# Attention and gated MLP on one core: PV placed beside score visits, output scaling and key masks on POOL, x held in two chunks

## The chip, the cores and the metric

The kernel runs on one core of a Trainium2 chip. A core has a matrix engine (TensorE, PE in the profile, with its weight loads as PEld), a vector engine (DVE), a scalar engine (ACT), a third elementwise engine (POOL), a queue engine (SP) that issues DMAs here, an on-chip memory of 128 partitions (SBUF) and eight accumulation banks of 128 x 512 fp32 (PSUM). The engines run their own instruction lists in order and wait for each other by semaphores. The metric is the device time of one execution in microseconds.

## The reference

There are 2,048 tokens of width 512. Two branches see the same x and are mixed per token by a gate. All tensors are bf16.

```python
x = A_x
g = sigmoid((x * gate_w).sum(-1))
a = A(x)          # 32 heads of 16, 4 segments of 512 tokens
b = B(x)          # gated MLP with 1,792 hidden units
out = g * a + (1 - g) * b

# A, per segment s, per head:
logits = q @ k.T * 16**-0.5 + causal mask      # 512 x 512, inside the segment
a_dot = softmax(logits) @ v
a_mem = (phi(q) @ M) / (phi(q) @ z + 1e-6)     # phi(t) = t + 1 for t > 0, else exp(t)
o = sigmoid(beta) * a_mem + (1 - sigmoid(beta)) * a_dot
M += phi(k).T @ v;  z += sum(phi(k))           # for the later segments
# then o @ wo

# B:
gate = x @ W_gate;  up = x @ W_up
return (gate * (gate > 0) * up) @ W_down
```

## The kernel before, in words

**Who decides the order.** `program` describes every piece of work as an `Op`: the engines that may do it, a cost for each, the resources that it reads and writes. `Sched.run` then walks a model of time: again and again it takes, of all queue heads, the one that can start first (queues have priorities, ties are broken by a seeded random number), puts it on its engine's list and notes the semaphore waits it needs. `Sched.emit` writes the lists out. So the order on each engine is fixed when the program is built, and a change of a cost, a buffer or a rule shifts all of it. PSUM accumulators are `Epoch`s: a bank is chosen when the first matmul of an epoch is placed and is free again when its readers are done.

**Projections** (`proj`, L671 and L673). Per segment, q and k are projected transposed (features on partitions), v token by token; 48 matmuls of 512 columns. DVE or ACT evicts them (L678, L682, L686, L699). The key masks (`kmask`, L690 on DVE, L691 on ACT) copy kT twice into `kp`, each time with half of the features of a head pair set to zero. For the memory, phi(q) and phi(k) are formed (L655 to L657) and phi(k) is transposed by DMA (L696).

**Score visits** (`quad`, L775). A group G holds 8 heads. Keys are taken in chunks of 64, and causality leaves chunk c with 512 - 64c query columns. A visit fills four PSUM banks of `psL` with 512 columns for each of four 32-row strips of TensorE: chunk 0 alone, chunks 1 and 7, 2 and 6, 3 and 5, and chunk 4 of two neighbouring groups. That makes 18 visits per segment. ACT takes the exponential of all 2,048 columns at once (L781) into one of eight blocks of `E` (seven in rotation, one kept for chunk 4), and POOL zeroes the triangles with four selects per visit (L786).

**PV** (L809). When all visits of a group are masked, 128 narrow matmuls multiply E by v, with a column of (1 + exp(beta)) for the denominator, into two banks. The half of v that sits on the other partitions is copied by DMA (`vsh`, L757). DVE transposes both banks into `Tn` (L819), takes the reciprocal (L827), multiplies in the gate (`rdg`, L829), scales into `adT` (`ad`, L831), transposes back (L834 or L836) and adds the memory part (L837) into `oT`. In the scheduler a PV belongs to a mode of TensorE of its own and is tied to a visit of the next group (`pair[0].gate = pes[k]`).

**Memory** (`mu`, L716 to L725; `nd`, L736 to L748): one update per segment, and four small matmul groups with a division per later segment.

**MLP** (`ffn`, L874 to L885; `outp`, L906 to L923). Per segment, 14 hidden blocks of 128: four gate and four up matmuls each, a relu (ACT L882 or DVE L883) and a product (DVE L885) into 16 slots `hT`. The output accumulates 14 matmuls with W_down (L913) and 4 with wo (L906) in one bank, and the eviction multiplies by 1 - g.

**x.** The transposed x, `xT`, holds all four chunks of 512 tokens. Chunk 0 is transposed by TensorE, chunks 1 to 3 come by transposing DMA (`load_x`, L506) on SP early on.

Of the kernel before, what the change touches and what calls it, by code (L numbers as in the profile page):

```python
# [15 lines left out]
MU_G = 1  # L16
PE_LAT = 175.0
SWITCH = 100.0
GATE_T = {1: 44000.0, 2: 90000.0, 3: 140000.0}

# [29 lines left out]
class Epoch:  # L50
    _n = 0

    def __init__(self, cls="mid", nb=1):
        self.nb = nb
        self.group = (self,)
        Epoch._n += 1
        self.res = f"ACCep{Epoch._n}"
        self.bank = None
        self.readers = []
        self.cls = cls  # L60


class Op:
    __slots__ = ("engs", "eng", "fns", "occs", "lat", "reads", "writes", "name", "dma", "nbytes", "mode", "ep", "role",
                 "after", "nbk", "port", "base", "preds", "stream", "idx", "start", "end", "done", "cidx", "gate", "nd")

    def __init__(self, alts, reads=(), writes=(), name="", lat=0.0, dma=False, nbytes=0, mode="f", ep=None, role=None):
# [18 lines left out]
        self.gate = None  # L86
        self.nd = 1
# [10 lines left out]
class Sched:  # L98
# [3 lines left out]
    def __init__(self, ndma=16, nbanks=4, seeds=(0,)):  # L102
        self.seeds = seeds
        self.jit = {}
        self.bank_ep = [None] * nbanks
# [88 lines left out]
    def pv_due(self):  # L194
        q = self.queues["pe"][self.pvq]
        while q[2] < len(q[1]) and q[1][q[2]].done:
            q[2] += 1
        if q[2] >= len(q[1]) or q[1][q[2]].gate is None:
            return 0
        t = self.now["pe"] + 500.0  # L200
        return q[1][q[2]].nbk if all(p.done and p.end <= t for p, _ in q[1][q[2]].preds) else 0

    def _bank_choice(self, op, e):
        cls, nb, n = op.ep.cls, op.ep.nb, len(self.bank_ep)
        idle = [p is None or all(r.done for r in p.readers) for p in self.bank_ep]
        if cls != "att":
            held = sum(not f and p.cls == cls for f, p in zip(idle, self.bank_ep))
            if held + nb > self.CAPS.get(cls, 2) or (n - sum(idle) + nb > n - max(self.pv_due(), 1) if nb == 1 else sum(idle) < (2 if self.relax else 3)):
                return None
        best = None  # L210
        for bi in range(n - nb + 1):
            if not all(idle[bi:bi + nb]):
                continue
            ft = max(self._bank_free(p, e) for p in self.bank_ep[bi:bi + nb])
            key = ft
            if nb == 1 and cls == "att" and n == 4:
                m = self.bank_ep[bi ^ 1]
                key += 0.0 if idle[bi ^ 1] or (m is not None and m.cls == "att") else 200.0
            if best is None or key < best[2]:
                best = (bi, ft, key)  # L220
        return best and best[:2]

# [6 lines left out]
    def ready(self, op, e):  # L229
        t0 = self.now[e]  # L230
        t = op.after
        if op.gate is not None:
            if self.mode != "r" and not op.gate.done:
                return None
            if sum(p is None or all(r.done for r in p.readers) for p in self.bank_ep) < op.nbk:
                return None
            t = max(t, sorted(self._bank_free(p, e) for p in self.bank_ep if p is None or all(r.done for r in p.readers))[op.nbk - 1])
# [5 lines left out]
        if op.ep is not None:  # L243
            if op.role == "w" and op.ep.bank is None:
                for rd in op.ep.readers:
                    for p, _ in rd.preds:
                        if p.ep is op.ep or p.cidx > op.cidx:
                            continue
# [3 lines left out]
                bc = self._bank_choice(op, e)  # L252
# [24 lines left out]
    def place(self, op, e, start):  # L277
        op.eng = e
        if op.ep is not None and op.role == "w" and op.ep.bank is None:
            for ep in op.ep.group:  # L280
                bi, _ = self._bank_choice(op, e)
# [45 lines left out]
        op.stream, op.idx, op.start, op.done = st, idx, start, True  # L327
        sn = dict(self.know[e])
# [7 lines left out]

    def jitter(self, op):
        seed = self.seeds[min(int(self.now["pe"] / 34000.0), len(self.seeds) - 1)]
# [5 lines left out]
    def _choose(self, e):  # L344
        heads = []
        for q in self.queues[e]:
# [6 lines left out]
            if rt is not None:  # L353
                pr = q[0]
                if e in ("dve", "act") and op.ep is not None and op.role == "r" and sum(p is None or all(r.done for r in p.readers) for p in self.bank_ep) < 2:
                    pr = min(pr, 0.5)
                heads.append((pr, rt, op))
        if not heads:
            return None
        now = self.now[e]  # L360
# [48 lines left out]
def plan(S, D, F):  # L409
    NT, KT, NF = S // 128, D // 128, F // 128  # L410
    return [
        ("xT", [128, KT, S], BF16), ("wq", [128, KT, 512], BF16), ("wk", [128, KT, 512], BF16), ("wv", [128, KT, 512], BF16),
        ("wo", [128, 4, 512], BF16), ("wg", [128, KT, F], BF16), ("wu", [128, KT, F], BF16), ("wd", [128, NF, 512], BF16),
        ("qT", [128, 8, 512], BF16), ("kT", [128, 4, 512], BF16), ("kp", [128, 5, 8, 128], BF16),
        ("phiq", [128, 4, 512], BF16), ("ek", [128, 4, 512], BF16), ("phik", [128, 4, 512], BF16), ("ttmp", [128, 2, 512], BF16),
        ("vaug", [128, 2, 4, 32, 17], BF16), ("vsh", [128, 4, 32, 17], BF16), ("E", [128, 8, 4, 512], BF16),
        ("Tn", [128, 2, 512], F32), ("adT", [128, 512], BF16), ("oTt", [128, 512], BF16),
        ("amem", [128, 2, 512], BF16), ("amemT", [128, 4, 512], BF16), ("oT", [128, 8, 512], BF16),
        ("hT", [128, 16, 512], BF16), ("rl", [128, 3, 512], BF16), ("osb", [128, 3, 512], BF16),
# [3 lines left out]
        ("rden", [128, 32], F32), ("rdg", [128, 32], F32), ("rdm", [128, 128], F32), ("pm8", [128, 8], F32), ("pm", [128, 2], F32), ("ident", [128, 128], BF16),  # L423
# [3 lines left out]
def build_kernel(nc, A_x, A_wq, A_wk, A_wv, A_wo, A_beta, W_g, W_u, W_d, gate_w, out):  # L427
# [5 lines left out]
    sc = Sched(seeds=(52936,98560,17166,30259,57195,44848,1710,92264))  # L433
    T = {}
    with contextlib.ExitStack() as stack:
        for name, shape, dt in plan(S, D, F):
            T[name] = stack.enter_context(nc.sbuf_tensor(name, shape, dt))
        PL = stack.enter_context(nc.psum_tensor("psL", [128, 4, 512], F32))
        PA = stack.enter_context(nc.psum_tensor("psA", [128, 4, 512], F32))
        for st in sc.streams:  # L440
            sc.sem[st] = stack.enter_context(nc.semaphore(f"s_{st}"))
        program(sc, nc, T, PL, PA, A_x, A_wq, A_wk, A_wv, A_wo, A_beta, W_g, W_u, W_d, gate_w, out, NSEG, KT, NF, NT, EPS, SCALE)
# [4 lines left out]

def program(sc, nc, T, PL, PA, A_x, A_wq, A_wk, A_wv, A_wo, A_beta, W_g, W_u, W_d, gate_w, out, NSEG, KT, NF, NT, EPS, SCALE):
    V = type("V", (), T)

# [24 lines left out]
    def A(ep):  # L475
        return PA[:, ep.bank, :] if ep.nb == 1 else PA[:, ep.bank:ep.bank + 2, :]

    def xt(c):
        return [f"xT{c}_{kt}" for kt in range(KT)] if c else [f"xT0_{i}" for i in range(6)]
# [24 lines left out]
    def load_x(c):  # L504
        for kt in range(KT):
            lsp.append(dma("sp", lambda e, c=c, kt=kt: e.dma_start_transpose(V.xT[:, kt, c * 512:(c + 1) * 512], A_x[0, c * 512:(c + 1) * 512, kt * 128:(kt + 1) * 128]),  # L506
                           1 << 17, occ=1280.0, writes=[f"xT{c}_{kt}"], name=f"ldx{c}_{kt}"))
# [39 lines left out]
    for b in range(4):  # L547
        ds.append(dve(lambda e, b=b: e.memset(PA[:, b, :], 0.0), 500, writes=[f"init{b}"], name=f"init{b}"))
# [100 lines left out]
    def qslot(s, G):  # L649
        return (s % 2) * 4 + G  # L650

    def phi(s, px, G, dst, dn, src, slot, rd, acts, sbs):
        xv, pv = src[:, slot:slot + 2, :], dst[:, G - 1:G + 1, :]
        wr = [f"{dn}{G - 1}", f"{dn}{G}"]
        acts.append(act(lambda e: e.activation(pv, xv, ACT.Exp), t_act(1024, False), reads=rd, writes=wr, name=f"{px}exp{s}_{G}"))  # L655
        sbs.append(dve(lambda e: e.tensor_scalar(V.ttmp[:, :, :], xv, 0.0, 1.0, ALU.max, ALU.add), 400, reads=rd, writes=["ttmp"], name=f"{px}ts{s}_{G}"))
        sbs.append(dve(lambda e: e.tensor_tensor(pv, pv, V.ttmp[:, :, :], ALU.min), 700, reads=wr + ["ttmp"], writes=wr, name=f"{px}phi{s}_{G}"))  # L657

    def proj(s):
        pes, evs, sbs, acts, sps = [], [], [], [], []  # L660
        tok = s * 512
# [17 lines left out]
        for G in range(4):  # L679
# [9 lines left out]
            for p in range(2):  # L689
                km = lambda e, kv=kv, p=p, ks=ks: e.tensor_scalar(V.kp[:, ks, :, 64 * p:64 * p + 64], kv, V.pm[:, p:p + 1], None, ALU.mult)  # L690
                ka = lambda e, kv=kv, p=p, ks=ks: e.activation(V.kp[:, ks, :, 64 * p:64 * p + 64], kv, ACT.Copy, scale=V.pm[:, p:p + 1])  # L691
                evs.append(sc.add(Op([("dve", km, 350)] + ([("act", ka, 720)] if s else []), reads=[f"kT{G}", "pm"], writes=[f"kp{ks}_{p}"], name=f"kmask{s}_{G}_{p}")))
            if s < NSEG - 1 and G % 2:
                phi(s, "k", G, V.ek, "ek", V.kT, G - 1, [f"kT{G - 1}", f"kT{G}"], acts, sbs)
                for g in (G - 1, G):
                    sps.append(dma("sp", lambda e, g=g: e.dma_start_transpose(V.phik[:, :, g * 128:(g + 1) * 128], V.ek[:, g, :]), 1 << 17, occ=1280.0, reads=[f"ek{g}"], writes=[f"phik{g}"], name=f"kT2{s}_{g}"))  # L696
# [62 lines left out]
    carry = []  # L759

    def att(s, between):
        pes, acts, pools, ds, pvs = [], [], [], [], []

        def quad(tag, parts, slot=None):

            e = slot
            if e is None:
                e = e_ctr[0]
                e_ctr[0] = (e + 1) % 7

            def fq(q):
                for G, c, o in parts:
                    for jj in range(4):
                        r = slice(32 * jj, 32 * jj + 32)
                        ins = q.matmul(PL[:, jj, o:o + 512 - 64 * c], lhsT=V.kp[r, kslot(s, G), c, :], rhs=V.qT[r, qslot(s, G), 64 * c:512], start=True, stop=True, tile_position=(32 * jj, 0), skip_group_check=True)  # L775
                return ins
            rd = sorted({f"kp{kslot(s, G)}_{p}" for G, _, _ in parts for p in range(2)} | {f"qT{qslot(s, G)}" for G, _, _ in parts})
            pes.append(pe(fq, 512 / 2.4 + 10.0 + 3.0 * (len(parts) - 1), reads=rd, writes=[f"bankL{b}" for b in range(4)], name=f"quad{s}_{tag}", mode="r"))
            pes[-1].after = 12000.0 + 3200.0 * qctr[0]
            qctr[0] += 1  # L780
# [248 lines left out]
```

## Time and profile before

| | us |
|---|---|
| median of 3 runs (lowest, highest) | 264.96 (264.82, 264.96) |
| span of the profiled execution | 263.0 |
| difference of the two | 1.96 |
| TensorE busy | 254.4 (97%) |
| ACT busy | 188.7 (72%) |
| DVE busy | 181.5 (69%) |
| POOL busy | 119.5 (45%) |

The profiled execution is reported by its span, from the first to the last instruction; no separate time is given for it. One core runs, and its granted TensorE clock is 1.000. In the lines of groups the columns are line, engine, operation, written tile and read tiles, shape and count, then busy time and mean length, then the idle time of the engine just before these instructions with what ended it. A matmul's length in the profile (380 ns) overlaps the next one's; the spacing of their starts says what one costs. A few per cent of matmul records are missing, and a missing one looks like a short idle time with the releaser "issue".

### The profile page before, as it was taken

Reading aid. Unit: us, or ns where it says so; the run is one execution under the profiler, and the core shown is the slowest. Engines: PE = TensorE matmul, PEld = TensorE weight load, DVE = VectorE, ACT = ScalarE, POOL = GpSimd, SP = SyncE. Lnnn points to the kernel's source line nnn. Section 1 sums busy time; section 2 is a strip of 40 time slices with the busy share of each in tenths; the row PEclk is TensorE's granted clock in tenths of the full one; section 3 lists DMA queues with packets and bytes.
Section 4 is the critical chain, followed back from the end, with each engine's and each line's share of the span. In section 5 each row is a group of like instructions: output and inputs, shape, how many; then the busy total and the mean of one; then the engine's idle time right before and its main releaser. Section 6 shows DMA issues by size and latency. Waiting matters only on the chain.

```text
span 263.0 us, 6637 instructions
## 1 busy us (share of the span) xinstructions
PE 254.4 (97%) x2714; PEld 113.1 (43%) x2748; DVE 181.5 (69%) x359; ACT 188.7 (72%) x167; POOL 119.5 (45%) x283
## 2 busy tenths in 40 slices
PE   7999999999999999999999999999999999999996
PEld 3444444434444443534444434444444434344444
DVE  5788887977886388876887954868582636657600
ACT  4597898599878789588886777787677657767021
POOL 3025544764545366764446265634344453535100
PEclk9999999999999999999999999999999999999999
DMA  6899666982041341510032320100034120000011
GB/s 182 223 379 209 135 83 80 286 146 57 20 106 23 75 68 44 82 40 4 0 87 64 80 62 23 21 4 2 0 92 55 22 60 22 0 2 1 4 40 40
DMA packets 34528, 19.23 MB, mean 73 GB/s; under 512 B 24001, under 2 KB 33986, under 8 KB 34498
## 3 DMA queue, kind: packets, MB, share of 16 engines
q1 hardware_dynamic: 34368, 18.80, 32.0%
q8 instruction: 21, 0.34, 0.6%
q14 instruction: 9, 0.07, 0.1%
q10 hardware_dynamic: 130, 0.01, 0.0%
HBM read 9.75 MB, written 2.11 MB: 45 GB/s over the span
## 4 chain that ended last, share of the span: by engine, by line
PE 94%; issue 2%; DVE 1%; DMA 1%; SPq 0%; ACT 0%; DVEq 0%
PE psA L874 37%; PE psA L913 19%; PE psA L673 11%; PE psL L775 9%; PE psA L809 7%; PE psA L906 5%; PE psA L671 5%; PE psA L736 1%; DMA hT<-in_A_x_dram 1%; PE psA L716 1%; DVE vaug L699 0%; SPq L484 0%; DVE phiq L657 0%; ACT xT L581 0%; DVE osb L922 0%
## 5 line engine op out<-in xcount | busy, mean ns | idle before, releaser
L786 POOL TENSOR_SCALAR_AFFINE_SELECT E<-E 64x256 bf16<-64x256 bf16 (+1 forms) x256 | 111.8, 446 | 122.2 <-ACT E L781 100.9
L781 ACT ACTIVATE E<-psL 128x2048 bf16<-128x2048 f32 x72 | 135.1, 1876 | 33.8 <-PE psL L775 31.1
L874 PE MATMUL psA<-xT,wg 128*128 128x512 bf16 x212 | 57.0, 380 | 1.9 <-issue 1.6
L874 PE MATMUL psA<-xT,wu 128*128 128x512 bf16 x219 | 58.0, 380 | 0.7 <-issue 0.5
L913 PE MATMUL psA<-wd,hT 128*128 128x512 bf16 (+2 forms) x229 | 52.2, 366 | 1.1 <-issue 1.0
L885 DVE TENSOR_TENSOR hT<-psA,rl 128x512 bf16<-128x512 f32 x56 | 38.2, 681 | 13.6 <-PE psA L874 11.3
L819 DVE STREAM_TRANSPOSE Tn<-psA 128x512 f32<-128x512 f32 x32 | 21.3, 696 | 20.0 <-PE psA L809 20.0
L913 PEld LDWEIGHTS psA<-wd,hT 128*128 128x128 bf16 x238 | 21.4, 98 | 23.7 <-issue 1.9
L874 PEld LDWEIGHTS psA<-xT,wu 128*128 128x128 bf16 x224 | 20.6, 98 | 25.3 <-issue 1.5
L874 PEld LDWEIGHTS psA<-xT,wg 128*128 128x128 bf16 x224 | 20.0, 98 | 24.9 <-issue 3.9
L775 PE MATMUL psL<-qT,kp 32*128 32x192 bf16 (+7 forms) x512 | 28.5, 287 | 0.0
L882 ACT ACTIVATE rl<-psA 128x512 bf16<-128x512 f32 x32 | 19.1, 597 | 10.2 <-PE psA L874 9.5
L775 PEld LDWEIGHTS psL<-qT,kp 32*128 32x128 bf16 x512 | 8.2, 92 | 29.9 <-issue 15.3
L923 ACT ACTIVATE osb<-psA,omg 128x512 bf16<-128x512 f32 (+1 forms) x12 | 8.1, 679 | 17.9 <-PE psA L906 14.0
L883 DVE TENSOR_SCALAR rl<-psA 128x512 bf16<-128x512 f32 x24 | 16.7, 696 | 3.2 <-PE psA L874 2.5
L809 PE MATMUL psA<-E,vaug 64*17 64x128 bf16 (+7 forms) x512 | 18.7, 283 | 0.0
L809 PE MATMUL psA<-E,vsh 64*17 64x128 bf16 (+7 forms) x512 | 18.3, 283 | 0.0
L673 PE MATMUL psA<-xT,wq 128*128 128x512 bf16 x62 | 16.2, 380 | 0.5 <-ACT xT L581 0.3
L906 PE MATMUL psA<-wo,oT 128*128 128x512 bf16 (+2 forms) x67 | 16.2, 366 | 0.2 <-issue 0.2
L673 PE MATMUL psA<-xT,wk 128*128 128x512 bf16 x61 | 16.0, 380 | 0.4 <-issue 0.3
L671 PE MATMUL psA<-wv,xT 128*128 128x512 bf16 x62 | 14.7, 380 | 0.3 <-issue 0.3
L809 PEld LDWEIGHTS psA<-E,vaug 64*17 64x17 bf16 x512 | 11.6, 86 | 6.0 <-issue 3.6
(76 smaller groups left out, 214.9 us busy)
## 6 DMA issues: line engine op xcount, KB each, us to landing
vsh<-vaug SPq DMA_DIRECT2D x8, 272.0 KB, 3.8
out_dram<-osb SPq DMA_DIRECT2D x15, 128.0 KB, 1.7
wg<-in_B_W_gate_dram SPq DMA_DIRECT2D x8, 224.0 KB, 5.7
wu<-in_B_W_up_dram SPq DMA_DIRECT2D x8, 224.0 KB, 5.9
wd<-in_B_W_down_dram SPq DMA_DIRECT2D x1, 1792.0 KB, 10.0
osb<-in_A_x_dram SPq DMA_DIRECT2D x12, 128.0 KB, 2.2
hT<-in_A_x_dram SPq DMA_DIRECT2D x4, 128.0 KB, 2.4
wq<-in_A_wq_dram SPq DMA_DIRECT2D x4, 128.0 KB, 2.8
```

The lines of the kernel that those rows point to most:

```text
L671: ins = e.matmul(A(ep)[:, :], lhsT=V.xT[:, kt, tok + col * 128:tok + (col + 1) * 128], rhs=w[:, kt, :], start=(kt == 0), stop=(kt == KT - 1))
L673: ins = e.matmul(A(ep)[:, :], lhsT=w[:, kt, col * 128:(col + 1) * 128], rhs=V.xT[:, kt, tok:tok + 512], start=(kt == 0), stop=(kt == KT - 1))
L775: ins = q.matmul(PL[:, jj, o:o + 512 - 64 * c], lhsT=V.kp[r, kslot(s, G), c, :], rhs=V.qT[r, qslot(s, G), 64 * c:512], start=True, stop=Tr ...
L781: acts.append(act(lambda a: a.activation(V.E[:, e, :, :], PL[:, :, :], ACT.Exp, scale=SCALE), t_act(2048), reads=[f"bankL{b}" for b in ran ...
L786: pools.append(pool(lambda g, ap=ap, base=base: g.affine_select(out=ap, in_=ap, compare_op=ALU.is_ge, fill=0.0, base=base, pattern=[[0, 4] ...
L809: ins = q.matmul(A(eps[p])[32 * jj:32 * jj + 17, 64 * c:512], lhsT=v[:, 8 * G + 2 * jj + p, :], rhs=V.E[r, e, jj, o:o + 512 - 64 * c], sta ...
L819: ds.append(dve(lambda e, p=p, ep=eps[p]: e.transpose(V.Tn[:, p, :], A(ep)[:, :]), t_dve(512), writes=[f"Tn{p}"], name=f"tr{s}_{G}_{p}", e ...
L874: ins = e.matmul(A(ep)[:, :], lhsT=w[:, kt, f * 128:(f + 1) * 128], rhs=V.xT[:, kt, c * 512:(c + 1) * 512], start=(kt == 0), stop=(kt == K ...
L882: evs.append(sc.add(Op([("act", lambda e, ep=eg, r=r: e.activation(V.rl[:, r, :], A(ep)[:, :], ACT.Relu), t_act(512)), ("dve", lambda e, e ...
L885: evs.append(dve(lambda e, ep=eu, r=r, hs=hs: e.tensor_tensor(V.hT[:, hs, :], A(ep)[:, :], V.rl[:, r, :], ALU.mult), t_dve(512), reads=[f" ...
L906: ins = e.matmul(A(ep)[:, 0:c1 - c0], lhsT=V.oT[:, o0 + G, i * 128:(i + 1) * 128], rhs=V.wo[:, G, c0:c1], start=st_ and G == 0, stop=sp_ a ...
L913: ins = e.matmul(A(ep)[:, 0:c1 - c0], lhsT=V.hT[:, slots[f], i * 128:(i + 1) * 128], rhs=V.wd[:, f, c0:c1], start=st_ and f == f0, stop=sp ...
```

## The change

It keeps the mathematics and the tile sizes and lays the work out anew.

- **Order of visits and PV.** Visits are built from a list: `ORDER` gives the chunks of each group, `UNITS` the size of a visit in units of 64 columns (18 visits of 8 units per segment, as many and as large as before). Chunk 4 stands at the end of an even group and at the start of an odd one. A PV may start when its gate, a visit, has been placed and either a new visit is due soon (`soon`), or none is left, or `STRICT` ns have passed; after it the scheduler stays with narrow work that is due (`HWAIT`) and asks the eviction engines to be near (`MWAIT`).
- **PSUM.** The two tensors `psL` and `psA` become one of eight banks. Visits still take banks 0 to 3; other work may use those between visits.
- **E** is one ring of 36 blocks of 512 columns, that is nine visits.
- **Key masks** of segments 1 to 3 run on POOL (before: DVE or ACT). Those of segment 0 stay on DVE.
- **Output scaling** `ad` runs on POOL in segments 0 to 2, on DVE in the last.
- **Tn** has four parts instead of two, so that two PVs can be in work; `rden` and `rdg` are doubled too.
- **xT** holds two chunks (`XR = 2`). Chunks 2 and 3 are loaded into the places of chunks 0 and 1 when these are done with; before, they were loaded early.
- **hT** has 20 slots instead of 16. The scheduler's seeds are new, and it draws some of its priorities per stretch of 8 us (`knob`).

```diff
-        ("xT", [128, KT, S], BF16), ...
+        ("xT", [128, KT, XR * 512], BF16), ...
-        ("vaug", ...), ("vsh", ...), ("E", [128, 8, 4, 512], BF16),
-        ("Tn", [128, 2, 512], F32), ...
+        ("vaug", ...), ("vsh", ...), ("E", [128, NBLK * 512], BF16),
+        ("Tn", [128, TNN, 512], F32), ...
...
-        PL = stack.enter_context(nc.psum_tensor("psL", [128, 4, 512], F32))
-        PA = stack.enter_context(nc.psum_tensor("psA", [128, 4, 512], F32))
+        PS = stack.enter_context(nc.psum_tensor("ps", [128, 8, 512], F32))
...
-    for c in range(2, NSEG):
-        load_x(c)
-        for t in lsp[-KT:]:
-            t.after = 22000.0 + 14000.0 * (c - 2)
...
+        if s + XR < NSEG:
+            lsp.clear()
+            load_x(s + XR)
+            sc.queue(0, list(lsp))
...
-                evs.append(sc.add(Op([("dve", km, 350)] + ([("act", ka, 720)] if s else []), ...
+                evs.append(sc.add(Op(([("pool", km, 660)] if s else [("dve", km, 350)]), ...
...
-            ds.append(dve(lambda e: e.tensor_tensor(av, Tv[:, :, :, 0:16], gv..., ALU.mult), 690, ...
+            ds.append((dve if s == NSEG - 1 or not ADP else pool)(lambda e: e.tensor_tensor(av, Tv[:, :, :, 0:16], gv..., ALU.mult), ...
...
-            if self.mode != "r" and not op.gate.done:
+            if self.mode != "r" and not self.relax and not (op.gate.done and self.now["pe"] > op.gate.start + STRICT) and not (op.gate.done and (self.next_visit() is None or self.soon(NEXT))):
                 return None
...
+        if e == "pe" and self.mode == "h":
+            near = [h for h in heads if h[2].mode == "h" and h[1] <= now + HWAIT] or [h for h in heads if h[2].mode in "rc" and h[1] <= now + HWAIT]
+            if not near and any(not t.done for t in self.mates) and min(self.now["act"], self.now["dve"]) < now + MWAIT:
+                return None
+            if near:
+                h = min(near, key=lambda h: h[1])
+                return h[2], h[1]
...
         at = {}
-        for G in range(4):
-            at |= quad(f"{G}A", [(G, 0, 0)])
-            at |= quad(f"{G}B", [(G, 1, 0), (G, 7, 448)])
...
+        todo = [(G, c, u) for G in range(4) for c in ORDER[s][G] for u in range(8 - c)]
+        i0 = 0
+        for k, units in enumerate(UNITS[s]):
...
+            visit(parts)
```

Some arguments in the diff are shortened to "...". In the changed kernel visits are L908, Exp L924, selects L930, PV L964, the transposes into Tn L974, `ad` L987, key masks L805, gate and up matmuls L1038, output matmuls L1070 and L1077.

More of the change, by code (lines that the diff above doesn't have):

```diff
@@ L16 @@
 MU_G = 1
+LAG = 0
+PAIR = 1
+LASTK = 17
+HWAIT = 250.0
+HEARLY = 3500.0
+MWAIT = 500.0
+PVR = 2
+NEXT = 1150.0
+TNN = 4
+STRICT = 6000.0
 PE_LAT = 175.0
@@ L889, in outp @@
         tiles, evs, sps = [], [], []
[L890 removed]
+        ot = [(s * 4 + G) % OTN for G in range(4)]
         for i in range(4):
```

363 lines of the change are left out of this document (254 added, 109 removed).

## The prediction

> **What bounds the kernel now.** I read the page first (busy shares, granted clock, the chain that ended last), then TensorE's timeline around three kinds of narrow block, then the groups of POOL and DVE by shape, last single lines with their shortest and longest instance.
>
> From the page:
>
> ```profile
> PE 254.4 (97%) x2714; PEld 113.1 (43%) x2748; DVE 181.5 (69%) x359; ACT 188.7 (72%) x167; POOL 119.5 (45%) x283
> ...
> PEclk9999999999999999999999999999999999999999
> ...
> PE 94%; issue 2%; DVE 1%; DMA 1%; SPq 0%; ACT 0%; DVEq 0%
> ...
> L786 POOL TENSOR_SCALAR_AFFINE_SELECT E<-E 64x256 bf16<-64x256 bf16 (+1 forms) x256 | 111.8, 446 | 122.2 <-ACT E L781 100.9
> L781 ACT ACTIVATE E<-psL 128x2048 bf16<-128x2048 f32 x72 | 135.1, 1876 | 33.8 <-PE psL L775 31.1
> L874 PE MATMUL psA<-xT,wg 128*128 128x512 bf16 x212 | 57.0, 380 | 1.9 <-issue 1.6
> ```
>
> TensorE is busy from end to end at the full clock and carries 94% of the last chain; idle time before its matmuls is put down to "issue", not to another engine. So a change gains only if it takes work or gaps out of TensorE's own stream, and loses wherever it makes that stream wait.
>
> TensorE's timeline: a score visit alone (62 to 64 us), a visit followed by PV (72 to 75 us), a PV alone (243 to 247 us); columns are start, length, instruction.
>
> ```profile
> 62.68 1.03 PE L874 MATMUL psA<-xT,wu 128*128 128x512 bf16 x4
> 63.64 0.40 PE L775 MATMUL psL<-qT,kp 32*128 32x384 bf16 x8
> 63.97 0.39 PE L874 MATMUL psA<-xT,wg 128*128 128x512 bf16 x1
> ...
> 72.62 1.03 PE L874 MATMUL psA<-xT,wu 128*128 128x512 bf16 x4
> 73.58 0.40 PE L775 MATMUL psL<-qT,kp 32*128 32x448 bf16 x8
> 73.91 0.39 PE L809 MATMUL psA<-E,vaug 64*17 64x512 bf16 x4
> ...
> 75.23 0.59 PE L671 MATMUL psA<-wv,xT 128*128 128x512 bf16 x2 [0.16 <-issue]
> ...
> 243.58 1.46 PE L913 MATMUL psA<-wd,hT 128*128 128x512 bf16 x6
> 244.97 0.39 PE L809 MATMUL psA<-E,vaug 64*17 64x512 bf16 x4
> ...
> 246.30 1.03 PE L913 MATMUL psA<-wd,hT 128*128 128x512 bf16 x4 [0.16 <-issue]
> ```
>
> A full matmul takes 0.216 us of the stream (start to start). Four from 62.68 end at 63.55; the stream goes on at 63.97: a visit alone costs 0.42. Four from 72.62 end at 73.48; the next shown matmul starts at 75.23. The 0.16 of "idle" before it is a lost record, not a wait: after the last PV the program issues 22 matmuls of L913, and from 246.30 to the next group at 250.83 only 21 fit. So the stream resumes at 75.01: visit plus PV 1.53. In the same way the PV alone costs 246.08 - 244.88 = 1.20. Separate they cost 0.42 + 1.20 = 1.62, together 1.53: a merge is worth 0.09 to 0.10 us.
>
> By shape, POOL and DVE, and two single lines (shortest/median/longest ns):
>
> ```profile
> L831 DVE TENSOR_TENSOR adT<-Tn,rdg 128x512 bf16<-128x512 f32 x16 | 11.4, 715 | 0.1
> L690 DVE TENSOR_SCALAR kp<-kT,pm 128x512 bf16<-128x512 bf16 x26 | 9.1, 378 | 1.6 <-PE psL L775 1.2 <-ACT kT L678 0.2
> L725 POOL TENSOR_TENSOR Mbd<-Mc,mumask 128x136 bf16<-128x136 f32 x12 | 5.6, 479 | 1.8 <-DVE ttmp L656 0.9 <-DVE Mc L721 0.9
> L534 POOL TENSOR_SCALAR_AFFINE_SELECT ident<-ident 128x128 bf16<-128x128 bf16 x1 | 0.3, 295 | 0.1
> L609 POOL TENSOR_TENSOR mumask<-mumask,eb 128x32 f32<-128x32 f32 x1 | 0.3, 262 | 0.0
> L829 DVE TENSOR_TENSOR rdg<-rden,gexpT x16: 203/217/445, 46.2 to 248.0; 128x32 f32<-128x32 f32 x16
> ```
>
> **TensorE's stream: -0.10 us.** Both programs issue 2,748 matmuls in the same shapes, and 72 visits of 2,048 logit columns (8 units of 64 query columns for each of 4 rows), so Exp has 72 equal instructions as before. What differs is order. In the old one 14 of 16 PVs already touch a visit (11 right behind it, one right ahead, two with the memory update between); two stand alone. In the new one 15 touch, mostly ahead of the visit; the one at the end stands alone. One merge more: -0.10. PV ahead of a visit is priced by its one case before, 47.61 to 49.27: two matmuls from 47.09 end at 47.52, and less the lost record the stream resumes at 49.05, again 1.53. The three memory updates stay next to narrow blocks: 0, between -0.15 and +0.15 each (a boundary is about 0.12: visit plus PV, 1.53, less 0.216 and 0.96 of columns, over three).
>
> **POOL: +33 us of work, 0 on the path.** Moved there are 24 key masks (segments 1 to 3; 18 were on DVE, 6 on ACT) and 12 output scalings `ad` (segments 0 to 2). No row shows either on POOL. Key mask, one tensor input, 512 elements: the selects give 295 ns at 128 and 446 at 256, so 446 + 2 x 151 = 0.75 us; ends 0.38 (DVE's) and 0.89 (twice the select). `ad`, two inputs: 262 at 32 and 479 at 136, 2.09 ns an element, so 1.26 us; ends 0.72 (DVE's) and 1.80 (479 x 512/136). I take the slopes, which come from POOL itself. 24 x 0.75 + 12 x 1.26 = 33: POOL goes from 119.5 to 153 us, 58%. What hides it is time between visits, so the tight place is a PV that waits for its masks. The chain is measured at the last PV of before: visit 240.22, Exp 240.67 to 242.55, four masks end 244.36, PV 244.97: 4.14 us of chain in 4.75. Counted out of the new order, the distance from the last needed visit to its PV falls to 4.74 us (segment 1, group 0; old order 7.0) and to 5.0 to 5.6 for six more; the old one has 6.4 or more but for its last. In segment 1, group 0, POOL has between the two last Exps (14 matmuls and a visit, 3.45 us) four masks, 1.8, and two key masks, 1.5: 3.3. There it fits, with 0.15 + 0.6 to spare; a stall begins when a key mask costs over 1.1 us, beyond the upper end. An `ad` behind schedule delays oT, which the output matmuls need many us later. Two pairs of Tn instead of one let the next PV be transposed without waiting for it. Cost 0.
>
> **DVE and ACT: 0.** DVE loses 18 x 0.378 + 12 x 0.715 = 15.4 us, ACT 6 x 0.714 = 4.3. Counted by tile, about 15 evictions and relus move from ACT to DVE (rl 32 to 22 on ACT): some 11 us back onto DVE. DVE ends near 177, ACT near 175; neither was the bound. If the cover goes, an eviction late by x holds a PSUM bank and stops the stream by x; before, no such wait was seen, and eight shared banks leave no fewer free than four fixed ones.
>
> The select's shortest instance takes 408 ns and its longest 969, rdg's 203 and 445: the two engines already hold each other up where DVE reads two SBUF inputs. The Trainium skill (GPSIMD Engine Reference, Specifications and Engine selection) says that POOL shares its SBUF interfaces with VectorE, that this hurts DVE instructions with two SBUF inputs or in a 2-port mode, and that two-input elementwise work belongs on VectorE. By the trace alone the sum keeps its zero; by that rule the new POOL work is paid for on DVE too, which is the second rival below.
>
> **x in two chunks: 0.** Eight transposing loads (chunks 2 and 3) leave 29 to 45 us on SP and wait until the last gate/up matmul on the slot's old chunk has ended. Between that matmul and the first projection of the new chunk lie, both times, 32 full matmuls, three visits and a PV: 32 x 0.216 + 1.53 + 2 x 0.42 = 9.3 us. Needed: 0.43 for the last matmul, 3 x 1.26 issue, landing 4.0 (shortest 2.6, longest 7.7, the latter behind all weights): 8.2, between 6.8 and 11.9. I take 8.2, since DMA is at 0 to 3 tenths there: hidden by 1.1. Behind the waiting loads on SP stand gate rows, keys for the memory update and the v shift, none due within 5 us.
>
> **E ring, tail: +0.04.** Nine blocks of E in rotation for seven plus one: no new wait. At the end 20 matmuls instead of 22 lie between the last PV and the first output matmul: 0.43 less cover for DVE's chain. That ended at 250.14 and the weight load came at 250.62; less 0.43, 0.05 us stays: 0 to 0.1 lost.
>
> **Sum.** -0.10 + 0.04: the profiled execution, span 263.0 us, would be 262.9; what lies outside the span (264.96 - 263.0 = 1.96, if that run was like the median) is untouched: 264.9 us. About 0.2%, 0.53 us, is what a measurement of this kernel tells from no change.
>
> **Rivals.**
> - POOL becomes late for PV (slower). With key masks of 1.5 and `ad` of 2.5 us, twice my prices, segment 1, group 0 has 4.8 us of work for 4.05: 0.75 late. Five PVs of segments 0 to 2 sit within 5.6 us of their visit: 5 x 0.6 = +3.0, 267.9. For: the shorter distances; selects stretched to 969. Against: it decides only above 1.1 us a key mask. Chance 0.09.
> - DVE held up by POOL's longer instructions. If each of 36 holds a two-input DVE instruction for half its length, 12 x 0.63 + 24 x 0.37 = 16 us more on DVE, 73% over all and some 86% from 32 to 147 us, where it is 80% busy; with three short bank waits of 0.4, +1.2: 266.1. For: rdg's 445. Against: the stream never waited with DVE at 80%. Chance 0.06.
> - x lands late: 6 us instead of 4.0 makes 10.2 for 9.3, twice 0.9: +1.8, 266.7. Against: quiet DMA. Chance 0.03.
> - The new order is worth more (faster): were the boundary between visit and PV free in the 15 pairs, -15 x 0.12 = -1.8: 263.1. Against: the one pair of that order cost the same 1.53. Chance 0.04.
> - That it changes next to nothing where it says most (PV beside visits was already so) is my forecast itself.
>
> **Numbers.** Forecast 0.78. Faster by over 0.2%: 0.04 and 0.01 of the forecast's edge, 0.05. Slower: 0.09 + 0.06 + 0.03, less 0.01 that stays within the bound, 0.17. Range 264.4 to 266.2: the forecast with its bounds (three updates, tail, up to 0.5) and the DVE case; left out are POOL, x and the faster case, 0.16.
>
> **What would show it.** Right: TensorE's waits still "issue" alone, span 262.7 to 263.2; POOL near 153 us with key mask 0.6 to 0.9 and `ad` 1.1 to 1.8; 72 Exps of 1,876. Wrong: TensorE or its weight loads waiting in front of PV for POOL, of a first q projection for DMA, or of gate/up for DVE; or a visit with PV at other than 1.53.

## The result, and the profile after

| | before | after |
|---|---|---|
| median of 4 runs each (lowest, highest), us | 264.96 (264.82, 265.21) | 268.35 (268.02, 268.97) |
| span of the profiled execution, us | 263.0 | 266.3 |

The ratio is 1.0137, 95% interval 1.0118 to 1.0156: slower by 3.4 us, where 264.9 was forecast and 266.2 was the upper end of the range. What happened is the mechanism of the first rival (POOL late for PV, 267.9).

From the page of the changed kernel, the lines that answer to those shown of before:

```profile
PE 259.5 (97%) x2748; PEld 113.7 (43%) x2748; DVE 179.1 (67%) x345; ACT 176.8 (66%) x145; POOL 164.3 (62%) x319
...
PEclk9999999999999999999999999999999999999999
...
PE 80%; POOL 15%; issue 2%; DVE 2%; ACT 1%; ACTq 0%; POOLq 0%; DVEq 0%
...
L930 POOL TENSOR_SCALAR_AFFINE_SELECT E<-E 64x256 bf16<-64x256 bf16 (+1 forms) x256 | 108.0, 435 | 78.6 <-ACT E L924 64.9
L1038 PE MATMUL ps<-xT,wg 128*128 128x512 bf16 x224 | 59.7, 380 | 0.0
L805 POOL TENSOR_SCALAR kp<-kT,pm 128x512 bf16<-128x512 bf16 x24 | 37.5, 1565 | 0.5 <-PE ps L908 0.5
```

The clock is the same. The last chain, 94% TensorE before, now runs for 15% through POOL, and POOL is busy for 164.3 us instead of the forecast 153. One group accounts for more than the difference: a key mask takes 1.565 us on the mean, where 0.75 was assumed (24 x 0.815 = 19.6 us); `ad` and the selects took less than assumed. (This profile holds all 2,748 matmuls, and no idle time of 0.16 stands before the gate and up matmuls any more: those of before were lost records, as assumed.)

The two moved operations, by instance (shortest/median/longest ns, first and last start):

```profile
L805 POOL TENSOR_SCALAR kp<-kT,pm x24: 1553/1556/1731, 31.5 to 177.8; 128x512 bf16<-128x512 bf16 x24
L987 POOL TENSOR_TENSOR adT<-Tn,rdg x12: 1047/1050/1430, 41.2 to 197.0; 128x512 bf16<-128x512 f32 x12
```

What TensorE's matmuls waited for (us in total, times, longest):

```profile
PE ps L964 <- POOL E L930: 3.2, 5, 1.0
PE ps L670 <- PEq L1183: 0.8, 1, 0.8
PE ps L788 <- ACT xT L695: 0.3, 1, 0.3
```

L964 is PV: 1,024 narrow matmuls on the page for 16 PVs, so 64 for each, half of what the description of the kernel before says. Five PVs wait for their masks, 3.2 us in all; the two other lines are the start of the kernel. No wait for a DMA is there, and none on DVE. Counted from starts (a full matmul every 0.216 us, then the boundary), the stream stands still for 0.29, 0.64, 1.08, 0.86 and 0.69 us, at 46.3, 61.7, 89.8, 104.3 and 164.5 us: 3.55 us, against 3.3 us between the spans.

The largest is the place that the prediction named, segment 1, group 0. POOL's timeline there (start, length, instruction, count, idle time before it and its releaser):

```profile
81.93 2.19 POOL L930 TENSOR_SCALAR_AFFINE_SELECT E<-E 64x256 bf16<-64x256 bf16 x5
84.44 1.56 POOL L805 TENSOR_SCALAR kp<-kT,pm 128x512 bf16<-128x512 bf16 x1 [0.33 <-PE ps L908]
85.96 0.41 POOL L930 TENSOR_SCALAR_AFFINE_SELECT E<-E 128x256 bf16<-128x256 bf16 x1
86.36 1.56 POOL L805 TENSOR_SCALAR kp<-kT,pm 128x512 bf16<-128x512 bf16 x1
87.88 2.58 POOL L930 TENSOR_SCALAR_AFFINE_SELECT E<-E 64x256 bf16<-64x256 bf16 x6
```

and TensorE's:

```profile
86.95 0.40 PE L908 MATMUL ps<-qT,kp 32*128 32x512 bf16 x4
87.28 1.47 PE L786 MATMUL ps<-wv,xT 128*128 128x512 bf16 x6
89.76 0.39 PE L964 MATMUL ps<-E,vaug 64*17 64x512 bf16 x4 [1.01 <-POOL E L930]
```

POOL works without a break from 84.44 us on: two key masks, and only then the masks that PV waits for. The six projection matmuls from 87.28 are done long before.

### The profile page after: what moved, and what is told of

Its sections match the earlier page's. It is cut to its first block, busy times and chain, and to the rows that moved or that the text cites. A ratio compares the mean times of both kernels' runs of the same rounds, so it can differ in the third digit from the quotient of the medians.

```text
span 266.3 us, 6663 instructions
## 1 busy us (share of the span) xinstructions
PE 259.5 (97%) x2748; PEld 113.7 (43%) x2748; DVE 179.1 (67%) x345; ACT 176.8 (66%) x145; POOL 164.3 (62%) x319
## 4 chain that ended last, share of the span: by engine, by line
PE 80%; POOL 15%; issue 2%; DVE 2%; ACT 1%; ACTq 0%; POOLq 0%; DVEq 0%
PE ps L1038 32%; PE ps L1077 16%; PE ps L788 9%; PE ps L908 7%; POOL E L930 7%; POOL kp L805 7%; PE ps L964 6%; PE ps L1070 5%; PE ps L786 3%; PE ps L851 1%; PE ps L670 1%; POOL adT L987 1%; ACT E L924 1%; POOL Mbd L840 1%; DVE ek L772 0%
## 5 line engine op out<-in xcount | busy, mean ns | idle before, releaser
L924 ACT ACTIVATE E<-ps 128x2048 bf16<-128x2048 f32 x72 | 135.0, 1875 | 43.8 <-PE ps L908 43.4
L930 POOL TENSOR_SCALAR_AFFINE_SELECT E<-E 64x256 bf16<-64x256 bf16 (+1 forms) x256 | 108.0, 435 | 78.6 <-ACT E L924 64.9
L1038 PE MATMUL ps<-xT,wg 128*128 128x512 bf16 x224 | 59.7, 380 | 0.0
L1038 PE MATMUL ps<-xT,wu 128*128 128x512 bf16 x224 | 58.9, 380 | 0.0
L1077 PE MATMUL ps<-wd,hT 128*128 128x512 bf16 (+2 forms) x238 | 55.1, 367 | 0.0
L1049 DVE TENSOR_TENSOR hT<-ps,rl 128x512 bf16<-128x512 f32 x56 | 38.4, 685 | 18.0 <-PE ps L1038 17.5
L805 POOL TENSOR_SCALAR kp<-kT,pm 128x512 bf16<-128x512 bf16 x24 | 37.5, 1565 | 0.5 <-PE ps L908 0.5
L1077 PEld LDWEIGHTS ps<-wd,hT 128*128 128x128 bf16 x238 | 21.4, 98 | 23.2 <-issue 2.6
L1038 PEld LDWEIGHTS ps<-xT,wg 128*128 128x128 bf16 x224 | 20.2, 98 | 25.6 <-issue 3.6
L974 DVE STREAM_TRANSPOSE Tn<-ps 128x512 f32<-128x512 f32 x32 | 21.2, 694 | 14.6 <-PE ps L964 14.6
L1038 PEld LDWEIGHTS ps<-xT,wu 128*128 128x128 bf16 x224 | 20.1, 98 | 25.4 <-issue 2.5
L908 PE MATMUL ps<-qT,kp 32*128 32x192 bf16 (+7 forms) x512 | 28.6, 287 | 0.0
L1047 DVE TENSOR_SCALAR rl<-ps 128x512 bf16<-128x512 f32 x34 | 23.2, 684 | 2.4 <-PE ps L1038 1.3
L964 PE MATMUL ps<-E,vaug 64*17 64x128 bf16 (+7 forms) x512 | 18.7, 283 | 3.2 <-POOL E L930 3.2
L908 PEld LDWEIGHTS ps<-qT,kp 32*128 32x128 bf16 x512 | 8.2, 92 | 26.2 <-issue 17.8
L964 PE MATMUL ps<-E,vsh 64*17 64x128 bf16 (+7 forms) x512 | 18.3, 283 | 0.0
L964 PEld LDWEIGHTS ps<-E,vaug 64*17 64x17 bf16 x512 | 11.9, 86 | 11.8 <-issue 6.1
L1070 PE MATMUL ps<-wo,oT 128*128 128x512 bf16 (+2 forms) x68 | 16.5, 367 | 0.0
```

Of the source, the lines that this page charges most:

```text
L908: ins = q.matmul(dst, lhsT=V.kp[r, kslot(s, G), c, :], rhs=V.qT[r, qslot(s, G), q0:q0 + w], start=True, stop=True, tile_position=(32 * jj, ...
L924: acts.append(act(lambda a: a.activation(V.E[:, base * 512:base * 512 + min(2048, 4 * W)], PF[:, 0:min(2048, 4 * W)], ACT.Exp, scale=SCALE ...
L930: pools.append(pool(lambda g, ap=ap, lim=lim, pat=pat: g.affine_select(out=ap, in_=ap, compare_op=ALU.is_ge, fill=0.0, base=lim, pattern=[ ...
L964: ins = q.matmul(A(eps[p])[32 * jj:32 * jj + 17, 64 * (c + u):64 * (c + u + n)], lhsT=v[:, 8 * G + 2 * jj + p, :], rhs=V.E[r, f:f + 64 * n ...
L974: ds.append(dve(lambda e, p=p, ep=eps[p]: e.transpose(V.Tn[:, 2 * (G % (TNN // 2)) + p, :], A(ep)[:, :]), t_dve(512), writes=[f"Tn{2 * (G ...
L1038: ins = e.matmul(A(ep)[:, :], lhsT=w[:, kt, f * 128:(f + 1) * 128], rhs=V.xT[:, kt, c % XR * 512:(c % XR + 1) * 512], start=(kt == 0), sto ...
```

## The experiments

All ratios are to runs of the kernel before on the same chip.

**The key mask as a two-input multiply, order untouched.** The same product, but the factor of each row is given as a second tensor, repeated along the row.

```diff
-                evs.append(sc.add(Op(([("pool", km, 660)] if s else ...
+                kt = lambda e, ...: e.tensor_tensor(V.kp[:, ks, :, 64 * p:64 * p + 64], kv, V.pm[:, p:p + 1].unsqueeze(2).to_broadcast([128, 8, 64]), ALU.mult)
+                evs.append(sc.add(Op(([("pool", kt, 660)] if s else ...
```

> The changed kernel with its order untouched; the 24 key masks on POOL multiply by the mask as a second input, spread over the columns, instead of a scalar per partition (same result). Theory P, the price: five PVs start late by 0.29 + 0.64 + 1.08 + 0.86 + 0.69 = 3.55 us because a key mask takes 1.56 us where 1.1 was the limit. The scaling, two inputs and 512 elements as well, takes 1.05; a mask of 1.05 makes 1.75 + 2.1 = 3.85 us of POOL work for the 4.05 in segment 1, group 0: no late PV, 264.6 to 265.2 us. Rival L, load and shared ports: POOL only falls from 164 to 152 us, a second input makes sharing with DVE worse, and the late PVs stay: 267 or more. If this form is no cheaper than the other: 268.3.

Measured: 264.85 us, ratio 1.0005 (0.9995 to 1.0016), span 263.0. The key mask by instance:

```profile
L807 POOL TENSOR_TENSOR kp<-kT,pm x24: 1032/1036/1043, 31.7 to 173.7; 128x512 bf16<-128x512 bf16 x24
```

POOL's timeline at the same place:

```profile
83.74 1.04 POOL L807 TENSOR_TENSOR kp<-kT,pm 128x512 bf16<-128x512 bf16 x1 [0.31 <-PE ps L909]
84.73 0.42 POOL L931 TENSOR_SCALAR_AFFINE_SELECT E<-E 128x256 bf16<-128x256 bf16 x1
85.11 1.04 POOL L807 TENSOR_TENSOR kp<-kT,pm 128x512 bf16<-128x512 bf16 x1
86.11 1.74 POOL L931 TENSOR_SCALAR_AFFINE_SELECT E<-E 64x256 bf16<-64x256 bf16 x4
```

The masks end at 87.85, PV starts at 87.99 without a wait, and no PV is late anywhere. Every other part of the change is still there, with the same lists of work on the engines: in this order the whole loss hangs on 0.52 us per key mask, and the rest of the change comes to nothing in sum.

**What sets the length of the key mask.** Twenty instructions, ten forms of two each, were put on POOL behind its last work; nothing else was changed, and the time, 276.13 us in one run, is longer because they run past the end.

```diff
+    probes = [lambda e: e.tensor_scalar(ksd, kd, V.pm[:, 0:1], None, ALU.mult),
+              lambda e: e.tensor_scalar(V.ek[:, 0, :], kc, V.pm[:, 0:1], None, ALU.mult),
...
+    for fn in probes:
+        for _ in range(2):
+            pr.append(pool(fn, 1500, ...))
+    sc.queue(9, pr)
```

> The changed kernel with the same order, and 20 more instructions on POOL behind its last select: the key mask as it is, the same with 512 and with 256 columns in one run, with fixed numbers instead of the per-partition scalar (one and two operations), with the mask as a second input (one run, and in runs of 64), an add of two tensors, a copy, a select of 512. The time grows where these run past the end, and is not the question. If the scalar per partition is dear: 1.56 with it in either layout, about 0.75 with a fixed number. If the runs of 64 columns are: 1.56 only there. If this kind of instruction is on POOL: 1.56 with any scalar, about 0.75 for copy and select.

By instance:

```profile
L1128 POOL TENSOR_SCALAR kp<-kT,pm x2: 1565/1565/1565, 248.5 to 250.2; 128x512 bf16<-128x512 bf16 x2
L1129 POOL TENSOR_SCALAR ek<-kT,pm x2: 1565/1582/1600, 251.8 to 253.6; 128x512 bf16<-128x512 bf16 x2
L1130 POOL TENSOR_SCALAR ek<-kT,pm x2: 925/926/927, 255.3 to 256.3; 128x256 bf16<-128x256 bf16 x2
L1131 POOL TENSOR_SCALAR ek<-kT x2: 1919/1926/1934, 257.4 to 259.4; 128x512 bf16<-128x512 bf16 x2
L1132 POOL TENSOR_SCALAR ek<-kT x2: 1491/1494/1497, 261.4 to 263.0; 128x512 bf16<-128x512 bf16 x2
L1133 POOL TENSOR_TENSOR ek<-kT,pm x2: 1040/1040/1040, 264.5 to 265.7; 128x512 bf16<-128x512 bf16 x2
...
L1135 POOL TENSOR_TENSOR ek<-kT x2: 1149/1150/1150, 269.0 to 270.2; 128x512 bf16<-128x512 bf16 x2
L1136 POOL COPY ek<-kT x2: 611/614/616, 271.4 to 272.1; 128x512 bf16<-128x512 bf16 x2
L1137 POOL TENSOR_SCALAR_AFFINE_SELECT ek<-ek x2: 614/614/615, 272.8 to 273.5; 128x512 bf16<-128x512 bf16 x2
```

The first line is the key mask as it is. The next writes one unbroken run (1.58), L1130 half of it (0.93), L1132 multiplies by a fixed number (1.49), L1131 applies two operations (1.93). So neither the layout nor the factor read per row makes it dear (a fixed number saves 0.07 us): the kind of instruction does, at (1565 - 926)/256 = 2.5 ns an element. The select goes from 0.41 at 256 elements to 0.61 at 512, 0.8 ns an element; a copy takes 0.61; two tensors multiplied 1.04, added 1.15.

**Length or kind: the two-input mask cut into pieces.** If the kind of instruction held POOL up in some way beyond its length, two-input pieces would do no harm. The order is untouched.

```diff
+                def kt(e, kv=kv, p=p, ks=ks):
+                    for c in range(0, 8, 4):          # in four: range(0, 8, 2), pieces of 2
+                        ins = e.tensor_tensor(V.kp[:, ks, c:c + 4, 64 * p:64 * p + 64], kv[:, c:c + 4], V.pm[:, p:p + 1].unsqueeze(2).to_broadcast([128, 4, 64]), ALU.mult)
+                    return ins
```

In two:

> The changed kernel with its order untouched; the late key masks are two-input multiplies on POOL (1.04 us whole, no late PV), here each cut into two halves. By the short two-input instructions in the trace of before (262 ns at 32 elements, 479 at 136) and 1,040 at 512, a half should take about 0.64, a whole mask about 1.27 us. Price theory (a PV is late by what the two key masks queued ahead of its masks take beyond its spare time): from the lateness measured at 1.556 us and two key masks each, 1.08, 0.86, 0.69 less 2 x 0.29 leave 0.50, 0.28, 0.11, and the others nothing: 265.3 to 266.1. Rival, that it is the kind of instruction (one tensor by a scalar of each row) which holds POOL up and not its length: 264.6 to 265.2.

In four:

> As the run with two halves, but in four quarters: about 0.43 us each, 1.7 us a mask, more than the 1.556 of the changed kernel, and with no instruction of the one-tensor kind. Price theory: the five late PVs are back, each 2 x 0.15 later than in the changed kernel: 268.4 to 270. Rival, kind of instruction: 264.6 to 265.5.

Measured: 265.05 us in two (ratio 1.0019, 1.0001 to 1.0036), 267.91 us in four (1.0111, 1.0093 to 1.0129). Pieces overlap a little, so what counts is the time from one mask's start to the next instruction's, at the tight place of segment 1, group 0 (in the timelines above 83.74 to 84.73 and 84.44 to 85.96):

| key mask | time taken on POOL, us | that PV is late by, us | expected from the second row at 2 us per us | all late PVs, us |
|---|---|---|---|---|
| two-input, whole | 0.99 | 0 | 0.01 | 0 |
| two-input, two halves | 1.13 | 0.29 | | 0.34 |
| two-input, four quarters | 1.43 | 0.86 | 0.89 | 3.06 |
| one-input (the changed kernel) | 1.52 | 1.08 | 1.07 | 3.55 |

What TensorE waited for with the mask in four pieces:

```profile
PE ps L968 <- POOL E L934: 2.7, 5, 0.8
```

The same five PVs are late again with no one-input key mask on POOL. At this place it is the length: two key masks stand ahead of this PV's masks, and beyond 0.99 us of each every nanosecond counts twice. At 62, 104 and 164 us the PVs are late by 0.50, 0.51 and 0.48 us with the mask in four pieces, where 2 x 0.09 less than in the changed kernel would give 0.46, 0.68 and 0.51: near the rule twice, off by 0.17 at 104 us. Both measured times lie below the expected ranges, because overlapping pieces take 1.13 and 1.43, not 1.27 and 1.7. The time in two halves, 265.05, would fit the rival as well; against the rival stand the PV that is late by 0.29 us there and the run with four pieces.

The PV near 46 us (segment 0, group 1) does not follow from lengths alone. In the changed kernel it is 0.29 us late, but POOL stands idle for 0.49 us just before the select that it waits for; the profile names a DVE instruction as what ended that, and what it was is open. With four pieces the PV is 0.71 us late, and one mask took 1.91 us instead of 1.47. Its last piece ran for 0.84 us (median 0.39) while DVE ran L772, which combines two tensors in SBUF and took 0.92 us itself (0.68 with whole two-input masks): side by side, both instructions were longer.

**Two-input masks in segment 2 alone, order untouched.**

```diff
-[("pool", km, 660)]
+[("pool", kt if s == 2 else km, 660)]
```

> The changed kernel, its order untouched, with the two-input key mask in segment 2 alone: those eight key masks run from 75 to 123 us, and stand ahead of two of the five late PVs (89.8 and 104.3 us, late by 1.08 and 0.86). Theory (each lateness is local, made by the key masks just ahead, and they add up): these two go, the three others (0.29, 0.64, 0.69) stay, so 268.35 - 1.94 = 266.4, between 266.0 and 266.8. Rival, that the stream makes up for a late PV or that lateness is passed on from one to the next: under 265.6 or over 267.3.

Measured: 266.74 us, ratio 1.0068 (1.0052 to 1.0084), span 265.0; TensorE's waits:

```profile
PE ps L965 <- POOL E L931: 1.4, 3, 0.6
```

The three that stay are late by 0.28, 0.64 and 0.69 us, as in the changed kernel. The stalls are local and add up.

**The scaling `ad` lengthened, order untouched.** In the kernel with two-input masks, `ad` is cut into four quarters.

```diff
+            def fad(e, n=4 if s < NSEG - 1 else 16):
+                for c in range(0, 16, n):
+                    ins = e.tensor_tensor(av[:, :, c:c + n], Tv[:, :, c:c + n, 0:16], gv[:, :, c:c + n].unsqueeze(3).to_broadcast([128, 2, n, 16]), ALU.mult)
+                return ins
```

> The changed kernel with the two-input key mask (264.85 us, no late PV), its order untouched, and the output scaling on POOL cut into four quarters of 128: by the quarters of the key mask (0.39 us) about 1.6 us instead of 1.05, so POOL has 12 x 0.55 = 6.6 us more work, 158 us, as much as lies between the runs of 154 and 164 that lost 0.3 and 3 us in late PVs. Theory (only what stands in POOL's queue ahead of a tight PV's masks counts, and a late scaling is needed by nobody soon): a scaling stands ahead of the masks of one of the five tight PVs, at 40.5 us, and POOL is idle for 1.0 us between the two: 264.6 to 265.4. Rival, that POOL's total decides: 266 to 267.

Measured: 265.04 us, ratio 1.0003 (0.9991 to 1.0015), POOL 156.1 us (4.2 more than with whole scalings, not 6.6), no late PV. POOL had more work than with the mask in two halves (154.4 us, 0.34 us of lateness), and lost nothing: where the work stands decides, not POOL's total.

**One part of the change taken back, with a new order.** Here the scheduler is given other engines for one operation, and lays everything out again. First the key masks back to DVE and ACT:

```diff
-[("pool", km, 660)] if s else [("dve", km, 350)]
+[("dve", km, 350)] + ([("act", ka, 720)] if s else [])
```

> The changed kernel with the key masks back on DVE or ACT, all else as changed (the scheduler orders anew; the distances from a visit to its PV stay as short, 4.7 to 5.6 us for nine PVs). Theory P: no PV waits for POOL, and the stream of TensorE, whose new order has one or two more boundaries (+0.25), gives 264.9 to 265.6. Rival D, that short distances alone make PVs late: 267 or more.

Measured: 265.47 us, ratio 1.0024 (1.0013 to 1.0035), no late PV; DVE 185.7, POOL 128.8 us. Then the scaling back to DVE, masks left on POOL:

```diff
-ADP = 1
+ADP = 0
```

> The changed kernel with the output scaling back on DVE in all segments, key masks still on POOL (ordered anew). Theory P: the key masks still take 1.56 and PVs stay late: 267 to 270. Rival A, that the scaling is what delays the masks: 265.5 or less, since 12 x 1.05 us leave POOL.

Measured: 268.92 us, ratio 1.0156 (1.0135 to 1.0178), span 267.0. Waits of TensorE:

```profile
PE ps L964 <- POOL E L930: 2.7, 3, 1.4
PE ps L964 <- DVE rdm L858: 0.7, 1, 0.7
```

With masks off POOL no PV is late; with the scaling off it three wait for masks, one for 1.4 us, and a fourth waits 0.7 us for DVE. Both agree with the price of the mask, but the orders are new, so the times are no measure of one part: the first stays 0.6 us above the kernel with two-input masks (265.47 to 264.85), without a wait that would account for it.

**The masks alone moved, in the kernel before.**

```diff
-                evs.append(sc.add(Op([("dve", km, 350)] + ([("act", ka, 720)] if s else []), ...
+                evs.append(sc.add(Op(([("pool", km, 660)] if s else [("dve", km, 350)]), ...
```

> The kernel before with one part of the change alone: key masks of segments 1 to 3 on POOL in their one-tensor form (1.56 us), scheduled as if they took 0.66. Counted out of its order, the last visit that a PV needs stands 6.2 us or more ahead of it (the last PV, 4.74, has no key mask near). Price theory with distance: chain 4.14 us, so 2.0 to 2.7 us to spare where the distance is 6.2 to 6.8; two key masks in between take 3.1: some PVs late by up to 1.1, 264.9 to 267.0. Rival, that the price alone does it and the shorter distances of the new order play no part: as the changed kernel, 267.9 or more. If it stays within 0.2% of before, the distances decide.

Measured: 274.27 us, ratio 1.0356 (1.0335 to 1.0378), span 273.1. That is far above the first theory; the rival's bound (267.9 or more) is open upwards, but the changed kernel itself loses only 3.4 us. To part price and order, the same lists of work with the two-input form of the first experiment:

> The kernel before with key masks of segments 1 to 3 on POOL, in the order of the run that cost 274.27 us, but as two-input multiplies (1.04 us instead of 1.56). Price theory: POOL's queue falls behind by 0.5 us less with each key mask; the late memory update with its PV at 48.7 us (2.27 late, two key masks in the five microseconds of POOL's work ahead of it and more further back) loses its wait or nearly so, and with it the wait for a bank behind it: 264.6 to 267. Rival, that in the old order any late PV costs a second wait, so that even a cheap key mask on POOL is dear there: 268 or more.

Measured: 269.72 us, ratio 1.0159 (1.0124 to 1.0195), span 268.7. Waits of TensorE in the first:

```profile
PE psA L716 <- POOL E L786: 2.7, 2, 2.3
PE psL L775 <- ACT E L781: 2.0, 4, 0.7
PE psA L874 <- DVE rdg L829: 1.8, 1, 1.8
PE psA L913 <- issue: 1.6, 1, 1.6
```

and in the second:

```profile
PE psA L875 <- DVE rdg L830: 1.7, 1, 1.7
PE psL L776 <- ACT E L782: 1.6, 3, 0.7
```

L716 is the memory update; the old kernel puts it ahead of its PV and gives it PV's waits, so the 2.7 us are late masks. They go with the cheaper mask, and the two times differ by 4.55 us. But 4.8 us over the kernel before stay, above the 267 of the theory, and masks are late there in one PV only, by 0.17 us: gate and up matmuls wait for DVE, and visits for the Exp of the visit before. These waits (3.3 us) belong to the order that the scheduler laid out once it was told that POOL takes the masks; where the rest goes was not found. So the rival (a cheap mask is dear too) was right on the time, and not for its reason, a second wait behind a late PV. And longer distances from visit to PV, 6.2 us and more here, gave no protection from the one-input mask: the memory update at 48.7 us, which waits for the masks of the PV behind it, was 2.27 us late after POOL had worked without a break from 31.1 to 47.6 us.

**The scheduler told the true price.** Two runs: the changed kernel with 1,560 ns for the one-input mask instead of 660, and the two-input kernel with 1,040 for the mask and 1,050 for `ad` instead of 1,360.

```diff
-[("pool", km, 660)]
+[("pool", km, 1560)]
```

> The changed kernel, key masks in their one-tensor form on POOL, with one number changed: the scheduler is told 1,560 ns for a key mask, as measured, and not 660. It lays the order out anew; counted from it, most PVs of segments 0 to 2 stand 7 to 12 us behind their last needed visit, one 4.2. Theory, that the harm is an order made with a wrong price: no PV over 1 us late, 264.6 to 265.9. Rival, that POOL at 62% can't take the key masks wherever they are put: 267 or more.

> The changed kernel with the two-input key mask, and the scheduler told what the traces show: 1,040 ns for a key mask (it was told 660) and 1,050 for the scaling on POOL (it was told 1,360). Nothing computed changes. Theory: TensorE's stream is the bound, the price was paid already in the run with the untouched order (264.85), so 264.5 to 265.3. Rival, that the order still has slack to gain from true prices: under 264.3. Against both: a new order may place some PV at the shortest distance again (4.1 us at one place by the count), up to 1 us late: 266.

Measured: 295.99 us (ratio 1.1153, 1.1098 to 1.1208) and 265.54 us (1.0023, 1.0013 to 1.0034). In the first, waits of TensorE and the stretches 90 to 128, 128 to 157 and 157 to 190 us (length; busy time and instructions of PE, PEld, DVE, ACT, POOL; granted clock; DMA):

```profile
PE ps L908 <- ACT E L924: 8.2, 6, 2.0
PE ps L1038 <- ACT E L924: 4.4, 2, 2.4
PE ps L851 <- ACT E L924: 4.0, 2, 2.0
```

```profile
90.00:128.00 38.00, 36.72 (x469) 15.53 (x473) 20.01 (x41) 24.59 (x18) 27.83 (x56) 1.00 0.16 33
128.00:157.00 29.00, 9.80 (x140) 3.33 (x141) 4.02 (x9) 16.60 (x10) 11.64 (x30) 0.62 0.25 56
157.00:190.00 33.00, 30.09 (x245) 12.80 (x246) 22.14 (x48) 15.12 (x24) 16.56 (x19) 0.86 0.20 33
```

The first meets the rival's 267 or more, but neither theory accounts for it: no PV waits for POOL. The order has almost no wide matmuls between 128 and 157 us, most visits wait for the Exp of the visit before, and TensorE's clock is lower as well. The second has two PVs late by 0.17 and 0.07 us and takes 0.7 us more than with the wrong prices (265.54 to 264.85), above the 265.3 that was expected; where the rest goes was not found. No version beat the kernel before; the best, two-input masks in the order of the change, equals it within the noise.

## Why the prediction was wrong

- **TensorE's stream** held: a PV that isn't late costs 1.52 us with its visit and 1.19 alone (1.53 and 1.20 assumed), a visit alone 0.43 (0.42). With the stalls removed the span is 263.0, against 262.9.
- **POOL, 0 on the path** is the step that failed, and in it one term: the key mask at 0.75 us, with 0.89 as the upper end, taken from the slope of the selects. It measured 1.556 us. Even as a select the slope was wrong (0.61 at 512 elements), but the fault is that a multiply by one number per row was priced as a select because both read one tensor. The upper end came from the same row, so it bounded nothing. The other moved price held: `ad` 1.05 for 1.26, between 0.72 and 1.80.
- **The tight place and its threshold** held for that place: a stall was to begin above 1.1 us a mask in segment 1, group 0; by the pieces it begins at 0.99 us from start to start (1.04 us by the profile's length). With the measured price that step gives (1.8 + 3.1) - 4.05 = 0.85 us; 1.08 came. But the prediction looked for tight places by the distance from visit to PV alone, and 1.6 of the 3.55 us came elsewhere: without a late PV (the run with two-input masks) the PVs that were late at 46.3, 61.7 and 164.5 us stand 7.9, 6.8 and 6.5 us behind their last visit.
- **The first rival** had the mechanism, and its price for the mask (1.5 for 1.56) was right. That it also had the count and nearly the size (five PVs, +3.0 us, for five and 3.55) is in part luck. The five that it meant stand within 5.6 us of their visit in segments 0 to 2; of these only two were late (1.08 and 0.86 us), three (groups 0 and 3 of segment 0, group 3 of segment 2) were not, and three others were. Its `ad` of 2.5 us did not come either. It was given 0.09 since its price stood outside the bounds.
- **DVE and ACT** held: 179.1 and 176.8 us (177 and 175), and no matmul waits for DVE. The second rival falls: with the two-input masks POOL has 32 us more work than before (151.9 for 119.5), 36 two-input instructions among it, and nothing is lost. The rule of the Trainium skill that weighed there, on shared SBUF interfaces (GPSIMD Engine Reference, Specifications), agrees with the one place in the run with four pieces where both engines' instructions were longer; in the times it cost nothing measurable.
- **x in two chunks** held: no matmul waits for a transposing load. **The tail**, 0.04 us, is too small to tell: 264.85 us with the two-input masks, 264.82 before.

## What to carry to other kernels

Price a moved operation by the same kind of instruction on the engine it moves to; if no row shows one, the bounds must reach over the dearest kind there, and the forecast must say what happens at that end. Check every place where the moved work stands in a queue ahead of something needed, not only where the distance is shortest. When a stall is local, test it by lengthening and shortening the suspect with the order untouched; a kernel whose scheduler lays out a new order for every changed cost moved by 0.6 to 31 us here for reasons of its own.

## What the runs showed of the hardware

On POOL a multiply of one tensor by a number per row takes 1.56 us for 512 bf16 elements, and the same product with the number given as a second tensor 1.04; a copy takes 0.61. On DVE the one-input form took 0.35 (median of before). The Trainium skill (GPSIMD Engine Reference, Engine selection) has two-input work on POOL about twice as slow as on VectorE and one-input work roughly at line rate. The trace has 1.05 against 0.715 for the two-input scaling, milder than that, and 1.56 against 0.35 for the one-input multiply: the order is the other way round.

In the run of 295.99 us the granted clock is 1.00 between 90 and 128 us, where TensorE is busy for 36.7 of 38 us. It is 0.62 between 128 and 157 us, where TensorE is busy for 9.8 of 29 us and no gap between matmuls exceeds 2.4 us. So the clock was lowered here without a longer gap; which share of gaps it takes was not tested.
